# Other streamed weight blocks in a recurrent attention kernel, and six late weight loads on another queue

## The chip, the core and the metric

The kernel runs on one core of a Trainium2 chip. The metric is the time of the whole program on the device, in microseconds. The core has a matrix engine (TensorE, PE), a vector engine (VectorE, DVE), an engine for activations and copies (ScalarE, ACT), a general engine (GpSimd, POOL) and one that mainly issues transfers (SyncE, SP). Each engine works through its own queue in order; between engines, semaphores say when something is ready. Transfers from and to the device memory are started by SP or by GpSimd and carried by 16 DMA engines that all queues share.

## What is computed

Two attention blocks read the same input x of 2048 rows and 640 columns, and a gate mixes them. Block A is ordinary sliding-window attention. Block B is recurrent: it goes through the sequence in 64 segments of 32 rows, and each segment needs 8 rows of memory that the segment before it produced. Cut to what matters:

```python
mem = mem0                                  # 8 rows
for s in range(64):
    h = concatenate([mem, x[:, 32 * s:32 * s + 32]])        # 40 rows
    q, k, v = h @ Wq, h @ Wk, h @ Wv        # 640 -> 32 heads x 192, each
    p = softmax(mask(q @ k.T * 192 ** -0.5))
    o = (p @ v) @ Wo                        # 32 x 192 -> 640
    mem = o[:, :8]
    outs.append(o[:, 8:])
b = concatenate(outs)
out = g * A(x) + (1 - g) * b                # g = sigmoid(sum(x * gate_w))
```

The weights Wq, Wk, Wv and Wo are 640 x 6144 or 6144 x 640 in bfloat16, some 7.9 MB each. All four together do not fit in the core's on-chip memory, and every one of the 64 steps needs all of them.

## The kernel before

The program has three parts. First `branch_A` computes the sliding-window block, and while it does, some weights of block B are loaded. Then a tail part (`Tail`) computes q, k and v for 8 of each segment's rows ahead of time (the steps carry 32 rows, 8 of memory and 24 of the segment); the results are stored to a scratch tensor `xin` and read back step by step. Last, `branch_B` runs the 64 recurrent steps, and these take most of the time.

Weights are cut in blocks named (kind, g, m). The kind is q, k, v or o; g from 0 to 3 is a group of 8 heads; m counts the slices of the contraction: 5 for q, k and v (384 KB a block), 6 for o (320 KB a block). That makes 84 blocks. The table `STREAMED` (L1077) says for each kind and group which m are streamed: these 22 blocks are loaded anew in every step, into a ring of six buffers (`RING`, tile `b_w`). The other 62 are resident: loaded once and kept. Among the resident ones, in the order of a list, the first 24 are loaded during `branch_A`, the next 27 during the tail part, and the last 11 very late (`LAST`): five of them at the end of the tail part, and six, called `held`, in step 0 of `branch_B` by `load_slow` (L757). All eleven are of kind o. The first five of the six `held` blocks go into the tile `hold`, which the tail part used to stage its stores; the sixth goes into a tile of its own. A block of o with m % 3 = 1 lies in two pieces in memory and takes two DMAs (L545 and L546), any other takes one.

A step runs in an order written out by hand in `STEP` (L636): `k0` stands for the five chunks of k, group 0, one for each m; `tk0` turns the result by transposes; `s0` are the scores of the group, `p0` turns the probabilities, `pv0` multiplies them with v, `oa0` and `ob0` are the first three and last three chunks of the output projection, and `m` turns the new memory rows for the next step. A chunk (L794, L989) is four matmuls on one block, and a chunk on a streamed block has to wait for its landing. TensorE follows `STEP` word for word. SP issues the loads of the streamed blocks in the order in which their chunks stand in `STEP`. A load can go out only when its ring buffer is free, that is when the block six places earlier in that order has been used.

The other engines' orders come from a planner, `Sched` (L420). Each operation is given to it with an engine, an estimated duration and latency, and what it reads and writes; at each point the planner takes the ready operation with the longest chain of work behind it. `sc.op("SP", ...)` and `sc.op("POOL", ...)` thus set in which queue an instruction goes out; on SP the order is that of creation.

GpSimd issues small loads in each step: `b_xg` (rows of q and k from `xin`, one a group), `b_xv`, `b_hT` and `b_ga`; it issues the stores of the results; and it copies pieces of `b_xg` into the tiles `b_QT`, `b_K` and `b_Kz`, which the scores read (L831, L850, L852).

In step 0 `load_slow(g)` is called just before the chunks of `v` of group g are created, and loads those `held` blocks that belong to group g. So nothing is loaded at v0 and v1, two blocks at v2, and four at v3, all on SP's queue.

Of the kernel before, what the change touches and what calls it, by code (L numbers as in the profile page):

```python
# [416 lines left out]
D = 640  # L417
# [273 lines left out]
def branch_B(ctx, tc, xin, mem0, weights, ring, c, omg_sb, ga_dram, b_dram, outf, hold, held, rest):  # L691
    nc = tc.nc
# [14 lines left out]
    sc = Sched({"rest": len(held)} | {t: n for t, (n, _) in sb.items()} | {t: n for t, (n, _) in kept.items()} | ps)  # L707
# [47 lines left out]
    slow = {}  # L755

    def load_slow(g):  # L757
        for i, u in enumerate(held):
            if u[1] == g:
                b = slow[u] = sc.buf("rest")  # L760

                def f(i=i, u=u):
                    if i < HOLD:
                        weights.load_held(hold, i, u, nc.sync)
                    else:
                        weights.load_resident(rest, u, nc.sync)
                sc.op("SP", 0.753 * 2 * D, 3000, f, writes=[b])

    hts = {0: load_x(0)}
    tp, m0 = sc.buf("tr"), sc.buf("w")  # L770
# [2 lines left out]
    def f_m0():  # L773
        t = tile_of(tp, [P, KT, MEM], BF, "tp0")
        for kt in range(KT):
# [4 lines left out]
          writes=[hts[0][0]], after=[hts[0][1]])  # L780
    made, tails = {}, {}

    def chunk(kind, s, g):
        if s == 0 and kind == "v":
            load_slow(g)
        hT = hts[s][0]
        b = sc.buf("mm")
        wb = pieces(kind, g)

        def f(kt):  # L790
            t = tile_of(b, [P, 512], FP32, f"ps_{kind}")
            w = w_of(kind, g, kt, wb)
            for j in range(4):
                nc.tensor.matmul(t[32 * j:32 * j + 32, 0:384], lhsT=tile_of(hT)[:, kt, :], rhs=w[:, j * 384:(j + 1) * 384],  # L794
                                 start=(kt == 0), stop=(kt == KT - 1), tile_position=(0, 32 * j))
        for kt in range(KT):
            sc.op("PE", 160, 330, lambda kt=kt: f(kt), reads=[hT] + [wb[m] for m in wb if m == kt], writes=[b], name=(kind, s, g, kt), mode=32)
        tok = sc.buf("vtok" if kind == "v" else "tok")

        def ev():  # L800
            src, dst = b["tile"][:, 0:384], tile_of(tok)[:]
            if kind == "v":
                src = src.rearrange("p (a e b) -> p a b e", a=2, b=3)
                dst = dst.rearrange("p (a b e) -> p a b e", a=2, b=3)
            nc.scalar.copy(dst, src)  # L805
        sc.op("ACT", 480, 50, ev, reads=[b], writes=[tok])
        made[kind, s, g] = tok
# [248 lines left out]
    with tc.manual_schedule():  # L1056
        parts = []
        for n in names:
# [15 lines left out]
LAST = 11  # L1074
HOLD = 5
DENSE = 8
STREAMED = {"q": ((1,), (2,), (0,), (0,)),  # L1077
            "k": ((1,), (1,), (1,), (1,)),
            "v": ((3,), (0, 4), (1, 4), (0, 4)),
            "o": ((2, 3), (2,), (2, 3), (2, 5))}  # L1080


@with_exitstack
def kernel(
# [31 lines left out]
    allp = [(k, g, m) for k in KINDS for g in range(4) for m in range(6 if k == "o" else 5)]  # L1116
    streamed = [(k, g, m) for k, g, m in allp if m in STREAMED[k][g]]
    weights = Weights(tc, B_Wq, B_Wk, B_Wv, B_Wo, streamed)
# [131 lines left out]
```

## Time and profile before

| | |
|---|---|
| median of 14 runs | 2013.04 us (2008.72 to 2022.04) |
| the profiled execution | 2015.26 us, its span on the core 2013.6 us |
| TensorE busy | 1907.2 us, 95% of the span |
| VectorE, ScalarE, GpSimd busy | 1011.6, 949.3, 719.5 us |
| moved by DMA | 618.99 MB, 307 GB/s over the span |
| queue of SP (q1), its share of the 16 DMA engines' time | 565.28 MB, 78.1% |
| queue of GpSimd (q0) | 47.74 MB, 8.1% |
| streamed blocks: issue to landing, median | 5.2 us (v and o), 5.8 us (q and k) |
| granted TensorE clock | 0.998 |

The profile is of one execution. The span runs from the first instruction to the last; the run's own time has 1.7 us around it. In a row of matmuls the first number after the bar is the busy time and the second the mean time of one in ns; "idle before" is the engine's idle time ahead of the row's instructions, with what ended it. Matmuls overlap in TensorE's pipeline and their ends are modelled, so a short wait can vanish from the idle column; the distance between two start times cannot. "DMA share" is the mean busy share of the 16 DMA engines.

### The profile page before, as it was taken

The numbers are of one execution on the slowest core, as the hardware profiler recorded it, in microseconds if no ns is written. First come the engines' busy times: TensorE is split into PE (matmuls) and PEld (weight loads), VectorE is DVE, ScalarE is ACT, GpSimd is POOL, SyncE is SP. The second block draws the span as 40 slices with busy tenths as digits, with TensorE's granted clock in tenths as the row PEclk, the third lists the DMA queues.
The fourth block names the chain that finished last, engine by engine and source line by source line (L and its number), as shares of the span: only waits on it lengthen the run. The fifth ranks groups of instructions, "written<-read, shape, count | busy, mean of one in ns | idle before, by whom it ended". The sixth has DMA issues, their size and how long they took to land.

```text
span 2013.6 us, 92179 instructions
## 1 busy us (share of the span) xinstructions
PE 1907.2 (95%) x39590; PEld 1412.0 (70%) x39590; DVE 1011.6 (50%) x3338; ACT 949.3 (47%) x1951; POOL 719.5 (36%) x2006
## 2 busy tenths in 40 slices
PE   8999999989999999999999999999999999999998
PEld 6878878656677666666666677777666666666665
DVE  5777853334444444444444444444444444444444
ACT  4888832334444444444444444444444444444443
POOL 5111121233334333333434333433333333333432
PEclk9999999999999999999999999999999999999999
DMA  4222159789999999999999999999999999999997
GB/s 156 79 83 78 35 148 325 213 300 341 345 365 364 358 344 352 352 353 344 360 357 358 338 355 360 365 360 357 360 356 350 353 353 341 342 361 355 362 348 270
DMA packets 260401, 618.99 MB, mean 307 GB/s; under 512 B 40552, under 2 KB 60176, under 8 KB 259984
## 3 DMA queue, kind: packets, MB, share of 16 engines
q1 hardware_dynamic: 228560, 565.28, 78.1%
q0 software_dynamic: 31424, 47.74, 8.1%
q8 instruction: 312, 5.11, 1.0%
q14 instruction: 105, 0.86, 0.1%
HBM read 583.49 MB, written 29.37 MB: 304 GB/s over the span
## 4 chain that ended last, share of the span: by engine, by line
PE 72%; DMA 20%; DVE 3%; ACT 2%; issue 1%; SPq 0%; POOL 0%; ACTq 0%; POOLq 0%; DVEq 0%
PE ps_o L989 14%; PE ps_q L794 10%; PE ps_k L794 10%; PE ps_v L794 9%; DMA b_w<-in_B_Wo_dram 8%; DMA b_w<-in_B_Wk_dram 5%; PE t_psum L605 5%; DMA b_w<-in_B_Wv_dram 4%; PE S_ps L874 3%; PE t_psv L623 3%; PE tr_q L818 2%; PE qk_ps L155 2%; PE tr_k L818 2%; DMA b_w<-in_B_Wq_dram 2%; PE ps_pv L956 2%; PE s_ps L251 2%
## 5 line engine op out<-in xcount | busy, mean ns | idle before, releaser
L794 PEld LDWEIGHTS <-b_hT 128*32 128x32 bf16 x15360 | 369.0, 96 | 237.4 <-issue 39.8
L989 PEld LDWEIGHTS <-b_OT 128*64 128x64 bf16 x6144 | 379.3, 110 | 38.2 <-issue 25.0
L794 PE MATMUL ps_k<-w_k,b_hT 128*32 128x384 bf16 x4096 | 256.6, 327 | 4.4 <-issue 1.2
L794 PE MATMUL ps_q<-w_q,b_hT 128*32 128x384 bf16 x4096 | 235.4, 327 | 1.5 <-issue 1.4
L989 PE MATMUL ps_o<-hold,b_OT 128*64 128x320 bf16 x2560 | 224.9, 300 | 0.2 <-issue 0.2
L989 PE MATMUL ps_o<-b_w,b_OT 128*64 128x320 bf16 x1792 | 207.5, 300 | 16.0 <-DMA b_w<-in_B_Wo_dram 14.6
L845 DVE TENSOR_TENSOR b_Kz<-tr_k,marks 128x256 bf16<-128x256 bf16 x256 | 108.0, 422 | 222.9 <-PE tr_k L818 218.8
L940 DVE TENSOR_TENSOR b_PTm<-PT_ps,marks 128x320 bf16<-128x320 f32 x256 | 125.9, 492 | 178.7 <-PE PT_ps L928 178.7
L254 ACT ACTIVATE pt<-s_ps 128x1024 bf16<-128x1024 f32 x180 | 183.3, 1026 | 47.8 <-PE s_ps L251 46.2
L967 ACT CAST b_OT<-ps_pv 128x480 bf16<-128x480 f32 x256 | 143.1, 559 | 126.0 <-PE ps_pv L963 126.0
L805 ACT CAST b_tok<-ps_k 128x384 bf16<-128x384 f32 x256 | 122.6, 479 | 168.1 <-PE ps_k L794 159.7
L794 PE MATMUL ps_v<-w_v,b_hT 128*32 128x384 bf16 x3328 | 201.7, 327 | 0.0
L805 ACT CAST b_vtok<-ps_v 128x384 bf16<-128x384 f32 x256 | 122.7, 479 | 130.9 <-PE ps_v L794 129.2
L989 PE MATMUL ps_o<-w_o,b_OT 128*64 128x320 bf16 x1792 | 171.4, 300 | 0.6 <-issue 0.6
L739 POOL DMA_DIRECT2D b_xg<-xin x256 | 142.3, 556 | 83.1 <-POOL b_QT L831 54.6
L827 ACT COPY b_QT<-tr_q 128x384 bf16<-128x384 bf16 x256 | 123.4, 482 | 88.2 <-PE tr_q L818 86.4
L805 ACT CAST b_tok<-ps_q 128x384 bf16<-128x384 f32 x256 | 123.0, 481 | 87.6 <-PE ps_q L794 87.2
L794 PE MATMUL ps_v<-b_w,b_hT 128*32 128x384 bf16 x1792 | 152.5, 330 | 9.6 <-DMA b_w<-in_B_Wv_dram 8.9
L850 POOL COPY b_K<-b_xg 128x64 bf16<-128x64 bf16 x256 | 60.9, 238 | 279.5 <-PE S_ps L874 278.8
L1018 DVE CAST b_hT<-mem_ps 128x16 bf16<-128x16 f32 x126 | 22.5, 178 | 262.2 <-PE mem_ps L1012 258.9
L1035 POOL DMA_DIRECT2D out_dram<-b_ga x126 | 62.7, 498 | 244.5 <-DVE b_ga L1030 233.9
L818 PEld LDWEIGHTS <-b_tok 128*64 128x64 bf16 x3072 | 108.3, 110 | 43.6 <-issue 27.3
(150 smaller groups left out, 3696.7 us busy)
## 6 DMA issues: line engine op xcount, KB each, us to landing
b_w<-in_B_Wv_dram SPq DMA_DIRECT2D x448, 384.0 KB, 5.2
b_w<-in_B_Wo_dram SPq DMA_DIRECT2D x448, 320.0 KB, 5.2
b_w<-in_B_Wk_dram SPq DMA_DIRECT2D x256, 384.0 KB, 5.8
b_w<-in_B_Wq_dram SPq DMA_DIRECT2D x256, 384.0 KB, 5.8
xin<-hold POOLq DMA_DIRECT2D x8, 1536.0 KB, 12.3
b_xg<-xin POOLq DMA_DIRECT2D x256, 48.0 KB, 4.9
w_q<-in_B_Wq_dram SPq DMA_DIRECT2D x16, 384.0 KB, 3.6
w_k<-in_B_Wk_dram SPq DMA_DIRECT2D x16, 384.0 KB, 3.6
```

Of the source, the lines that this page charges most:

```text
L254: nc.scalar.activation(out=pt, in_=sp[:], func=ACT.Exp, scale=scale)
L605: self.nc.tensor.matmul(pt[:, bb, :], lhsT=w[kt][:, c:c + P], rhs=self.xTb[:, kt, t0:t0 + hs * MEM], start=(kt == 0), stop=(kt == KT - 1))
L739: sc.op("POOL", 540, 5000, lambda: nc.gpsimd.dma_start(tile_of(b)[:].rearrange("p i b t -> p (i b t)"), xin[s, :, c:c + 192]), writes=[b])
L794: nc.tensor.matmul(t[32 * j:32 * j + 32, 0:384], lhsT=tile_of(hT)[:, kt, :], rhs=w[:, j * 384:(j + 1) * 384], start=(kt == 0), stop=(kt == ...
L805: nc.scalar.copy(dst, src)
L818: nc.tensor.transpose(t[64 * a:64 * a + 64, k, :], tok["tile"][:, c:c + 64], ident[:], tile_position=(0, 64 * a))
L827: nc.scalar.copy(dst, tq["tile"][:].rearrange("p b (j t) -> p b j t", t=SEG))
L845: nc.vector.tensor_tensor(out=tile_of(Kz)[:, :, :, 0:SEG], in0=src, in1=mk_z.unsqueeze(1).unsqueeze(3).to_broadcast([P, 4, 2, SEG]), op=AL ...
L940: nc.vector.tensor_tensor(out=tile_of(PTm)[:], in0=src.to_broadcast([P, 2, 4, L]), in1=mk_m.unsqueeze(1).unsqueeze(3).to_broadcast([P, 2, ...
L967: sc.op("ACT", 560, 50, lambda: nc.scalar.copy(tile_of(OT)[:, 0:12 * L], o["tile"][:, 0:12 * L]), reads=[o], writes=[OT])
L989: nc.tensor.matmul(t[64 * h:64 * h + 64, 0:D // 2], lhsT=OT["tile"][:, c:c + 64], rhs=w, start=(g == 0 and m == 0 and n == 0), stop=(g == ...
L1035: sc.op(eng, 500, 3000, lambda h=h: queue.dma_start(half(outf, h), mine(tile_of(ga), h)), reads=[ga])
```

## The change

Two edits. The table of streamed blocks gets other entries. There are 22 a step before and after, of which q now has 6 (4 before), k 3 (4), v 6 (7) and o 7 (7). And `load_slow` puts the six held blocks on GpSimd's queue instead of SP's: three of them when v0 is created and three when v1 is, each after the last operation that was created before it; the estimates given to the planner change with it. As the table of o changes, the six held blocks are (o,2,3), (o,2,4), (o,3,0), (o,3,1), (o,3,3) and (o,3,4); before, they were (o,2,4), (o,2,5) and the same four of group 3.

```diff
     def load_slow(g):
-        for i, u in enumerate(held):
-            if u[1] == g:
-                b = slow[u] = sc.buf("rest")
-
-                def f(i=i, u=u):
-                    if i < HOLD:
-                        weights.load_held(hold, i, u, nc.sync)
-                    else:
-                        weights.load_resident(rest, u, nc.sync)
-                sc.op("SP", 0.753 * 2 * D, 3000, f, writes=[b])
+
+        half = -(-len(held) // 2)
+        last = sc.ops[-1]
+        for i, u in list(enumerate(held))[g * half:(g + 1) * half]:
+            b = slow[u] = sc.buf("rest")
+
+            def f(i=i, u=u):
+                if i < HOLD:
+                    weights.load_held(hold, i, u, nc.gpsimd)
+                else:
+                    weights.load_resident(rest, u, nc.gpsimd)
+            sc.op("POOL", 560, 6000, f, writes=[b], after=[last])
...
-STREAMED = {"q": ((1,), (2,), (0,), (0,)),
-            "k": ((1,), (1,), (1,), (1,)),
-            "v": ((3,), (0, 4), (1, 4), (0, 4)),
-            "o": ((2, 3), (2,), (2, 3), (2, 5))}
+STREAMED = {"q": ((4,), (3,), (1, 4), (0, 3)),
+            "k": ((1,), (4,), (), (4,)),
+            "v": ((2,), (4,), (1, 4), (0, 4)),
+            "o": ((0, 3), (2,), (2, 5), (2, 5))}
```

## The prediction

> **What bounds the kernel now.** I read the page's slices first, then the chain of waits, then the windows of single steps, then TensorE's order of time inside a step.
>
> ```profile
> DMA  4222159789999999999999999999999999999997
> GB/s 156 79 83 78 35 148 325 213 300 341 345 365 364 358 344 352 352 353 344 360 357 358 338 355 360 365 360 357 360 356 350 353 353 341 342 361 355 362 348 270
> ...
> PE 72%; DMA 20%; DVE 3%; ACT 2%; issue 1%; SPq 0%; POOL 0%; ACTq 0%; POOLq 0%; DVEq 0%
> ...
> L989 PE MATMUL ps_o<-b_w,b_OT 128*64 128x320 bf16 x1792 | 207.5, 300 | 16.0 <-DMA b_w<-in_B_Wo_dram 14.6
> ```
>
> From slice 9 on, the 64 recurrent steps run: TensorE and the DMA engines are both full, and the chain goes over PE with 20% on the landings of b_w, the streamed weight blocks. Four windows give step 0, steps 1 and 2, and a step in the middle:
>
> ```profile
> core 0: us, PE busy (x) PEld busy (x) DVE busy (x) ACT busy (x) POOL busy (x), PEclk, DMA share, GB/s
> 420.00:450.60 30.60, 24.72 (x521) 17.51 (x521) 11.19 (x41) 11.53 (x26) 8.57 (x28) 0.94 1.00 363
> 450.60:475.90 25.30, 23.51 (x526) 16.92 (x526) 11.83 (x43) 11.01 (x25) 9.65 (x28) 1.00 0.98 347
> ...
> 1018.60:1043.00 24.40, 23.61 (x526) 16.49 (x526) 11.82 (x43) 10.59 (x24) 9.66 (x28) 1.00 0.99 352
> ```
>
> The idle column understates the waits, because matmul ends are modelled. The start times show them:
>
> ```profile
> 1020.38 0.66 PE L794 MATMUL ps_q<-w_q,b_hT 128*32 128x384 bf16 x12
> 1020.87 0.34 PE L794 MATMUL ps_k<-w_k,b_hT 128*32 128x384 bf16 x4
> 1021.32 0.35 PE L794 MATMUL ps_k<-b_w,b_hT 128*32 128x384 bf16 x4
> 1021.48 0.67 PE L794 MATMUL ps_k<-w_k,b_hT 128*32 128x384 bf16 x12
> ```
>
> A chunk of four matmuls follows the one before it after 0.16 us; the chunk on b_w, k(1,1), came after 0.45: 0.29 us of waiting with no idle time in the row. I measured every chunk so, start to start, over steps 2 to 63, against its own 5th percentile. A step has a mean of 24.68 us: a floor of **23.43** (all 5th percentiles), **0.89** lost ahead of the 22 streamed chunks, 0.36 elsewhere. The fastest five steps took 23.7. So 0.89 x 63 = 56 us is all that block placement could ever give.
>
> **Part 1: the streamed blocks at other places.** Bytes first: both tables stream 15 blocks of 384 KB and 7 of 320 KB a step, and none of the o blocks streamed in either has m % 3 = 1, so one DMA each. SP issues the same 22 DMAs, in the order of use. What changes is the spacing. Block i can be issued only when block i-6 has been used, so its time is the PE time between these two uses, its **window**. From the issue (about 0.25 us after the use ends) to the landing takes 5.2 to 5.8 us by the median, 3.7 at least: a window under about 6 has little to spare. I laid both tables on the floor's times (a chunk 0.163, of o 0.272 us). Per place: window before > after, and the block's measured slack (landing to use, median) with the mean wait before:
>
> - o(2,3) > o(2,5): 5.18 > 5.72; slack 0.04, wait 0.247
> - k(1,1) > k(1,4): 5.92 > 6.40; 0.06, 0.150
> - v(3,4) stays: 5.57 > 6.12; 0.28, 0.079
> - v(2,4) stays: 5.53 > 6.02; 0.47, 0.067
> - o(1,2) stays: 5.38 > 6.24; 0.52, 0.029
> - q(0,1) > q(0,4): 6.09 > 6.57; 0.61, 0.037
> - q(1,2) > q(1,3): 6.82 > 6.44; 0.63, 0.045
> - k(2,1) > q(2,4): 7.24 > 6.51; 1.18, 0.010
> - k(3,1) > q(3,3): 7.17 > 6.20; 1.29, 0.014
> - v(1,0) > k(3,4): 6.97 > 5.95; 1.53, 0.005
> - o(2,2), o(3,5), o(3,2), k(0,1) keep 5.83, 5.56, 6.04, 5.93; waits 0.059, 0.067, 0.001, 0.025
>
> The rest keeps a slack near 1. I add the change of window to the slack and read the new wait off the same list (slack 0.5 to 0.6 went with about 0.03, 0.3 with about 0.07). Gains: o(2,5) 0.22, k(1,4) 0.12, v(3,4) 0.07, v(2,4) 0.06, o(1,2) and q(0,4) 0.03 each: 0.53. Losses: q(1,3) at slack 0.25 0.035, q(2,4) at 0.45 0.04, q(3,3) at 0.32 0.055, k(3,4) at 0.51 0.035: 0.165. Net **-0.37 us a step if the windows were independent**.
>
> They aren't: a wait that goes also shortens the windows that held it. 0.37 us less per step is 0.37 x 6/22 = 0.10 us less in each window. Nine places then stand under 0.6 of slack; near there the list loses about 0.25 us of wait per us of slack: 9 x 0.10 x 0.25 = +0.22. What is left is **-0.15 us a step, x 63 = -9 us**. Ends: no feedback, -23; all given back because the transfers are the bound, 0. I take -9.
>
> A rule speaks against any gain. The Trainium skill, page "DMA: Bandwidth & Descriptors", section "Bandwidth" (Where 436 GB/s comes from), says that loads from HBM are held by a limit of about 358 GB/s per core. Slices 10 to 38 average 354 GB/s, which over 24.68 us is 8.74 MB a step; at 358 the step could not go below 24.4, a gain of at most 0.27 us a step, 17 in all. The trace goes past it: slices reach 365, and a 384 KB block that had a backlog ahead of it landed 0.97 us after its predecessor by the median, 405 GB/s. By the row the floor stays PE's 23.43. My -9 fits under both; the far end is -17 by the rule and -23 by the row. The row decides, but I let the rule pull the low end in a little.
>
> **Part 2: the late loads.** Six late o blocks (1.97 MB, nine DMAs, as three have m % 3 = 1) went out on SP ahead of the ring loads of v2 and v3 in step 0:
>
> ```profile
> 436.97 0.35 PE L794 MATMUL ps_v<-b_w,b_hT 128*32 128x384 bf16 x4 [1.20 <-DMA b_w<-in_B_Wv_dram]
> 438.07 0.35 PE L794 MATMUL ps_v<-b_w,b_hT 128*32 128x384 bf16 x4 [0.43 <-DMA b_w<-in_B_Wv_dram]
> 443.43 0.35 PE L794 MATMUL ps_v<-b_w,b_hT 128*32 128x384 bf16 x4 [2.58 <-DMA b_w<-in_B_Wv_dram]
> 444.71 0.51 PE L794 MATMUL ps_v<-b_w,b_hT 128*32 128x384 bf16 x4 [0.28 <-DMA b_w<-in_B_Wv_dram]
> ```
>
> That is 4.49 us of waiting, of the 5.35 by which step 0 (30.03) exceeds the mean. On GpSimd's queue they no longer stand ahead of ring loads in one queue, and are issued some 2 us earlier, at v0 and v1. But six blocks of 320 KB take 6 x 0.83 = 5.0 us of the DMA engines (0.83 is the landing distance of such blocks), and the window of step 0 above shows a DMA share of 1.00: there is no hole to put them in. The two queues' packets will mix, ring loads run slower while both are full, and the waits spread over o(0,3), v(2,4), o(1,2) and v3 with the same sum. So **0**, between -4.5 (all hidden) and +5 (late and doubled).
>
> SP is rid of nine issues of 0.33 to 1.2 us. GpSimd takes them on, four behind the evacuation of k2 and five behind the copies of tk2, each near this row:
>
> ```profile
> L739 POOL DMA_DIRECT2D b_xg<-xin x256: 537/556/581, 304.7 to 1988.3; - x128
> ```
>
> 9 x 0.556 = 5.0 us of GpSimd, once. Behind them stand its copies of xg into K02, Kz and QT, which S of the next group reads; GpSimd waited 1.5 to 3.9 us for S_ps before each group of copies in step 0, so four or five issues (2.2 or 2.8 us) are mostly covered. Without that cover: +2 us. The skill's page "SBUF — State Buffer", section "SBUF: two separate sides", warns of exactly this move: descriptors of a GpSimd DMA wait for VectorE's two-port instructions, 620 ns becoming 3100. By it the nine would take 28 us and starve the scores of step 0, about +15. The row says no: 256 issues beside a VectorE busy 47% of a step took 581 ns at most. I take the row. The destination (hold) was last read by stores issued at 421.8 at the latest, which land some 4.3 us later, before 428, so that wait costs nothing.
>
> What lies ahead of step 0 moves one q and one v block between ring and resident loads with equal bytes: 0, +/-1.
>
> **Sum**, against the profiled execution (span 2013.6, 2015.26 with what lies around it): -9 + 0 + about 1 for GpSimd = -8. The median of 14 runs, 2013.04, is 2.2 below that execution; taken off the median: **2005**.
>
> **Rivals.**
> - *A, the transfers are the bound* (share 0.98 to 0.99 in each step): bytes equal, so every wait removed returns elsewhere. For it: the share. Against it: steps of 23.7 us happen. Time: 2013, +/-4.
> - *B, no feedback*: -0.37 x 63 = -23, cut to -19 by the bandwidth: 1994. Against it: landings have a backlog in most cases, so slack is shared.
> - *C, slower: the new crowd in q2 to k3.* q(2,1), q(2,4), v(0,2), q(3,0), q(3,3), k(3,4) pull six blocks into 4.9 us of PE time where five stood, and two pairs are 0.5 us apart while a block takes 0.97. xg, out and ga transfers of GpSimd pass in the same stretch. If q(2,4), q(3,3) and k(3,4) each wait as k(1,1) did (0.15) and feedback takes half of the gain, the step is 3 x 0.15 + 0.035 - 0.53/2 = +0.22 worse before its own feedback, some +0.1 after: 2019. It decides from a mean wait of about 0.12 at each of the three.
> - That the step table does nothing is excluded: SP and PE read it directly.
>
> **Chances.** The likeliest case 0.50, A 0.25, B 0.08, C 0.17. Its own range is 1998 to 2011. For 8 in 10 I go from 1995 (most of B) to 2016 (A, the edge of C). A measurement here tells 0.2%, 4 us, from nothing. Faster: 0.45 of the likeliest, B, and a little of A: 0.57; same 0.26; slower 0.17.
>
> **What would show it.** Right: mean step near 24.5, waits ahead of o(2,5) and k(1,4) under 0.06, total ahead of streamed chunks near 0.74, step 0 again near 30 but with its waits smaller and more of them; nine GpSimd issues near 0.55 us. Wrong: waits over 0.12 at q(2,4), q(3,3), k(3,4) (C); a mean step at 24.7 with waits moved to o(2,2) and o(3,5) (A); GpSimd issues over 1 us or S_ps waiting for GpSimd in step 0; step 0 under 28 or over 33 us.

## The result, and the profile after

The changed kernel takes 1997.66 us (median of 10 runs, 1989.93 to 2002.47); the kernel before, run beside it, 2012.87. The ratio is **0.9921**, 95% interval 0.9904 to 0.9938: 15 us, 0.8% faster. The forecast was 2005, 8 us faster.

The page of the changed kernel (lines after L757 have moved by two: L794 is L796 now, L989 is L991). First the chain of waits by engine, then two groups of matmuls on streamed blocks:

```profile
PE 77%; DMA 14%; DVE 3%; ACT 2%; issue 2%; SPq 0%; POOL 0%; ACTq 0%; POOLq 0%; DVEq 0%
...
L991 PE MATMUL ps_o<-b_w,b_OT 128*64 128x320 bf16 x1792 | 205.9, 300 | 0.9 <-DMA b_w<-in_B_Wo_dram 0.7
...
L796 PE MATMUL ps_q<-b_w,b_hT 128*32 128x384 bf16 x1536 | 130.9, 329 | 9.8 <-DMA b_w<-in_B_Wq_dram 8.3
```

The row of the q chunks before:

```profile
L794 PE MATMUL ps_q<-b_w,b_hT 128*32 128x384 bf16 x1024 | 87.5, 332 | 3.1 <-DMA b_w<-in_B_Wq_dram 2.9
```

Landings fell from 20% of the chain to 14%. The o chunks on streamed blocks waited 16.0 us in the row of before and 0.9 now; the q chunks, of which half as many again are streamed, waited 3.1 and now 9.8. The list of waits has a second place where the same loss stands, and it is easily misread: weight loads (PEld) that waited for "issue", that is for nothing the profile names. Before (who waited for what: us in total, times, longest):

```profile
PEld L794 <- issue: 39.8, 84, 1.7
...
PEld L989 <- issue: 25.0, 51, 1.7
```

After:

```profile
PEld L796 <- issue: 44.1, 83, 2.0
...
PEld L991 <- issue: 4.3, 11, 0.8
```

I looked up which matmul follows each of these waits from step 1 on: of 64.8 us on both lines before, 53.8 stand directly ahead of a chunk on b_w; of 48.4 after, some 34. I take these for late landings too, seen at the weight load instead of the matmul; with half the bytes (below) they are gone. For o they have nearly gone (25.0 to 4.3), for q, k and v they have not.

Start to start, which counts both kinds, as in the prediction (steps 2 to 63, each chunk against its own 5th percentile, us a step):

| | mean step | floor | ahead of streamed chunks | elsewhere | step 0 |
|---|---|---|---|---|---|
| before | 24.68 | 23.43 | 0.89 | 0.36 | 30.03 |
| after | 24.43 | 23.41 | 0.55 | 0.47 | 31.64 |

62 steps x 0.25 = 15.7 us less; step 0 is 1.6 longer, step 1 1.2 shorter, and the part ahead of step 0 0.8 shorter: together 16.1 of the 16.3 by which the profiled span shrank (2013.6 to 1997.3). So in these two executions the whole gain lies in the steady steps.

Step 0 is another picture. The windows of steps 0 and 1 of the changed kernel, with the columns of the prediction's:

```profile
420.30:452.00 31.70, 25.52 (x530) 17.80 (x531) 11.39 (x42) 11.09 (x25) 12.88 (x34) 0.95 0.97 354
452.00:476.10 24.10, 23.17 (x529) 16.77 (x530) 11.81 (x44) 11.00 (x25) 9.61 (x29) 1.00 0.98 345
```

GpSimd is busy for 12.88 us in step 0 (8.57 before), and the DMA share has fallen from 1.00 to 0.97. TensorE's order of time says why; these two starts follow waits that the kernel before did not have:

```profile
433.56 0.21 PE L876 MATMUL S_ps<-b_K,b_QT 128*64 128x40 bf16 x2 [0.82 <-POOL b_QT L833]
...
439.78 0.21 PE L876 MATMUL S_ps<-b_K,b_QT 128*64 128x40 bf16 x2 [2.33 <-POOL b_QT L833]
```

And GpSimd's order of time, where the bracket is its idle time:

```profile
430.93 0.55 POOL L542 DMA_DIRECT2D hold<-in_B_Wo_dram  x1 [4.02 <-issue]
...
435.34 0.54 POOL L542 DMA_DIRECT2D hold<-in_B_Wo_dram  x1
435.86 0.54 POOL L545 DMA_DIRECT2D w_o<-in_B_Wo_dram  x1
437.17 0.54 POOL L546 DMA_DIRECT2D w_o<-in_B_Wo_dram  x1 [0.77 <-DMA hold<-in_B_Wo_dram]
438.22 0.54 POOL L739 DMA_DIRECT2D b_xg<-xin  x1 [0.52 <-DVE b_PTm L942]
438.75 0.25 POOL L852 COPY b_K<-b_xg 128x64 bf16<-128x64 bf16 x1
438.92 0.48 POOL L854 COPY b_Kz<-b_xg 64x32 bf16<-64x32 bf16 x2
439.46 0.26 POOL L833 COPY b_QT<-b_xg 128x96 bf16<-128x96 bf16 x1
```

The scores of group 3 needed the copies at 437.4; they stood behind six issues, the last of the first half and the five of the second, and behind a load of xg; TensorE waited until 439.78. In the kernel before, the late loads went out on SP from here on:

```profile
429.16 0.33 SPq L545 DMA_DIRECT2D hold<-in_B_Wo_dram  x1
```

### The profile page after: what moved, and what is told of

Same layout as the page of the kernel before. It is cut to its first block, busy times and chain, and to the rows that moved or that the text cites. A ratio compares the mean times of both kernels' runs of the same rounds, so it can differ in the third digit from the quotient of the medians.

```text
span 1997.3 us, 92168 instructions
## 1 busy us (share of the span) xinstructions
PE 1899.5 (95%) x39590; PEld 1398.9 (70%) x39590; DVE 1011.6 (51%) x3338; ACT 949.0 (48%) x1951; POOL 721.9 (36%) x2015
## 4 chain that ended last, share of the span: by engine, by line
PE 77%; DMA 14%; DVE 3%; ACT 2%; issue 2%; SPq 0%; POOL 0%; ACTq 0%; POOLq 0%; DVEq 0%
PE ps_o L991 19%; PE ps_v L796 10%; PE ps_q L796 9%; PE ps_k L796 9%; DMA b_w<-in_B_Wq_dram 6%; PE t_psum L605 4%; DMA b_w<-in_B_Wv_dram 4%; PE S_ps L876 3%; PE ps_pv L958 3%; PE t_psv L623 3%; PE qk_ps L155 3%; PE tr_q L820 2%; DMA b_w<-in_B_Wk_dram 2%; PE tr_k L820 2%; PE s_ps L251 2%
## 5 line engine op out<-in xcount | busy, mean ns | idle before, releaser
L796 PEld LDWEIGHTS <-b_hT 128*32 128x32 bf16 x15360 | 372.6, 96 | 242.6 <-issue 44.1
L991 PEld LDWEIGHTS <-b_OT 128*64 128x64 bf16 x6144 | 363.0, 111 | 30.9 <-ACT b_OT L969 9.6
L796 PE MATMUL ps_k<-w_k,b_hT 128*32 128x384 bf16 x4352 | 235.3, 328 | 3.6 <-issue 0.4
L991 PE MATMUL ps_o<-hold,b_OT 128*64 128x320 bf16 x2560 | 236.1, 301 | 0.5 <-issue 0.5
L796 PE MATMUL ps_q<-w_q,b_hT 128*32 128x384 bf16 x3584 | 224.5, 328 | 0.5 <-issue 0.5
L796 PE MATMUL ps_v<-w_v,b_hT 128*32 128x384 bf16 x3584 | 213.7, 328 | 4.3 <-issue 2.1
L991 PE MATMUL ps_o<-b_w,b_OT 128*64 128x320 bf16 x1792 | 205.9, 300 | 0.9 <-DMA b_w<-in_B_Wo_dram 0.7
L739 POOL DMA_DIRECT2D b_xg<-xin x256 | 141.8, 554 | 89.1 <-POOL b_QT L833 53.8
L991 PE MATMUL ps_o<-w_o,b_OT 128*64 128x320 bf16 x1792 | 169.4, 299 | 0.4 <-issue 0.4
L893 ACT ACTIVATE S_ps<-S_ps 128x160 f32<-128x160 f32 x256 | 75.1, 294 | 137.6 <-DVE S_ps L890 136.6
L796 PE MATMUL ps_q<-b_w,b_hT 128*32 128x384 bf16 x1536 | 130.9, 329 | 9.8 <-DMA b_w<-in_B_Wq_dram 8.3
```

The costliest lines, as they stand in the source:

```text
L739: sc.op("POOL", 540, 5000, lambda: nc.gpsimd.dma_start(tile_of(b)[:].rearrange("p i b t -> p (i b t)"), xin[s, :, c:c + 192]), writes=[b])
L893: nc.scalar.activation(out=view(), in_=view(), func=ACT.Exp, scale=scale)
L991: nc.tensor.matmul(t[64 * h:64 * h + 64, 0:D // 2], lhsT=OT["tile"][:, c:c + 64], rhs=w, start=(g == 0 and m == 0 and n == 0), stop=(g == ...
```

## The experiments

The theory: the gain comes from the table alone, by the windows; the moved loads bring nothing. The rivals: the loads carry part of it; the transfers are the bound and placement only moves the waits. All ratios are to the kernel before on the same chip, with their 95% intervals. In a profile of one execution the mean step varies by some 0.1 us, so medians decide, and the places only show where. How far one profile carries can be seen where two kernels have the same table (us a step, as in the table above; e8 is the changed kernel with another queue for the late loads):

| | table | mean step | floor | ahead of streamed chunks | elsewhere |
|---|---|---|---|---|---|
| before | old | 24.68 | 23.43 | 0.89 | 0.36 |
| e2 | old | 24.72 | 23.44 | 0.99 | 0.29 |
| changed | new | 24.43 | 23.41 | 0.55 | 0.47 |
| e1 | new | 24.59 | 23.37 | 0.82 | 0.40 |
| e8 | new | 24.44 | 23.33 | 0.55 | 0.56 |

The direction is the same in all: the mean of the three minus the mean of the two is -0.22 us a step, of which -0.30 ahead of streamed chunks, +0.15 elsewhere and -0.07 in the floor. The size of a single term is not: e1's execution took 8 us more than its median. Its row of the o chunks has 5.3 us of waiting where the changed kernel has 0.9, a third of the 16.0 before:

```profile
L989 PE MATMUL ps_o<-b_w,b_OT 128*64 128x320 bf16 x1792 | 205.8, 300 | 5.3 <-DMA b_w<-in_B_Wo_dram 4.4
```

The part ahead of step 0 varies too, without any difference in the program: it took 420.4 us in e7 and 426.1 in the same kernel again.

**The table alone**, and **the loads alone**. The change is taken apart at its seam; in e1 `load_slow` is as before, in e2 the table is:

```diff
 e1:  "o": ((2, 3), ...) -> ((0, 3), (2,), (2, 5), (2, 5)), q, k, v likewise
 e2:  nc.sync -> nc.gpsimd in load_slow, as in the change
```

> The new table of streamed blocks alone, the late loads on SP's queue as before. Windows theory (the waits are set by the spacing of the uses, and all of the gain comes from the table): mean step near 24.43 us as after, streamed waits near 0.55 a step, step 0 back near 30.0 instead of 31.6, with no wait of the scores for GpSimd's copies; about 1996 us, ratio 0.9915 to the kernel before. Rival (the moved loads carried part of the gain): slower than the changed kernel, over 2000 us.

> The late loads on GpSimd's queue alone, the old table. Windows theory: step 0 near 31.6 us with the scores of groups 2 and 3 waiting for GpSimd's copies, all later steps as before (24.7), so 1 to 2 us slower than before, near 2014.5. Rival (the moved loads carried part of the gain): faster than before by 3 us or more.

The table alone: 1999.61 us, ratio 0.9925 (0.9900 to 0.9949), the same as the whole change. The loads alone: 2013.53, ratio 0.9993 (0.9978 to 1.0008), no difference that can be told. Step 0 was 30.53 and 30.83 us. In e2 the scores waited again for GpSimd, 1.05 and 1.37 us:

```profile
435.00 0.21 PE L876 MATMUL S_ps<-b_K,b_QT 128*64 128x40 bf16 x2 [1.05 <-POOL b_QT L833]
...
440.27 0.21 PE L876 MATMUL S_ps<-b_K,b_QT 128*64 128x40 bf16 x2 [1.37 <-POOL b_QT L833]
```

The rival that the loads carry part of the gain falls. The 1 to 2 us of loss that e2 was to show are below what these intervals resolve.

**Only the o row**, and **only the q, k and v rows** of the new table, loads on SP:

```diff
 e3:  q, k, v as before; "o": ((0, 3), (2,), (2, 5), (2, 5))
 e4:  q, k, v as after;  "o": ((2, 3), (2,), (2, 3), (2, 5))
```

> Only the o row of the new table; loads on SP. Windows theory: o(2,3)'s wait of 0.25 us goes (o(2,5) below 0.05), v(3,4) falls from 0.08 to 0.02, but q(1,2) loses 0.54 us of window (6.82 to 6.28) and waits about 0.15; net -0.15 to -0.2 us a step before other places take some back, so -6 to -10 us. Rival A (the transfers are the bound): the step stays at 24.7, the waits appear elsewhere, 0 +/- 3 us.

> Only the q, k and v rows of the new table; loads on SP. Windows theory: k(1,4) waits 0.03 to 0.05 instead of 0.15, v(2,4) and o(1,2) little, q(2,4) about 0.17 as after, o(2,3) still about 0.25, net -0.1 us a step, -4 to -7 us; with e3 it adds up to the -15 us of the whole table. Rival A: 0 +/- 3 us. If the places share one pool of slack, e3 and e4 each give clearly more, or less, than their part of the sum.

The o row alone: 2002.68 us, ratio 0.9934 (0.9912 to 0.9956). The other three rows: 2014.43, ratio 0.9994 (0.9976 to 1.0013). Eight of the ten moved blocks bring nothing together that can be told (5 us less to 3 us more); the two o blocks bring nearly everything. The profile of e4 shows the balance that the theory expected, at smaller sizes: k(1,4) waits 0.06 (k(1,1) had 0.15), q(2,4) 0.10 (k(2,1) had 0.01), and o(2,3) still 0.16. Its -4 to -7 us were too much. That the new o blocks merely load faster than those that they replace can be excluded: in the changed kernel, o blocks with a backlog ahead of them landed 0.90, 0.86, 0.82 and 0.82 us after their predecessor for m = 0, 2, 3 and 5 (medians).

**One o block at a time**:

```diff
 e10: "o": ((2, 3), (2,), (2, 5), (2, 5))      # o(2,3) to o(2,5)
 e11: "o": ((0, 3), (2,), (2, 3), (2, 5))      # o(0,2) to o(0,0)
```

> One block alone is moved: o(2,3) to o(2,5), everything else as before. Windows theory with little feedback (a wait that goes stays gone): the 0.2 to 0.25 us ahead of o(2,3) vanish, q(1,2) loses 0.54 us of window and keeps some slack, so the step gets 0.15 to 0.2 us shorter, -9 to -13 us, nearly all that the whole table brought. With the feedback of the prediction (0.6 of each gain given back elsewhere): -4 to -6 us. Rival (several places share the gain, v(3,4) by the release of o(0,0) among them): under half of the -12.6 us of the whole o row.

> One block alone is moved: o(0,2) to o(0,0), everything else as before. It releases its ring buffer 0.55 us earlier for v(3,4), whose window grows from 5.57 to 6.12; its own window falls from 6.25 to 5.71. The whole o row gave -12.6 us and o(2,5) alone -4.2. Windows theory: v(3,4) stops waiting (0.08 to 0.02) and lands earlier, so o(2,2) and o(2,3) behind it in the DMA queue land earlier too; -0.1 us a step, -4 to -8 us, and the two edits add up. Rival (they do not add up; o(0,0) alone does nothing): 0 +/- 3 us.

Both ratios are 0.9979 (0.9964 to 0.9995, and to 0.9993): 4 us each, 1 to 7. So by the medians o(2,3), with a wait of 0.25 us a step (16 us in all) the worst place of the kernel before, yielded about a quarter of that when it was moved alone. The profile of e10 does not bear out so much feedback: its waits did go to the last o places (o(2,5) 0.055, o(3,2) 0.052, o(3,5) 0.054), but its mean step is 24.50, 0.18 less than before, which is 11 us over 62 steps; its part ahead of step 0 took 426.5 us, 5.3 more than before. How much one place gives back when it is moved alone is therefore not settled. The sum of the two, 0.42%, with 0.15% of uncertainty on each, lies just below the interval of e3 (0.44 to 0.88%); whether the two help each other beyond their sum is not settled.

e11 missed in a way that teaches more than its time. Moving o(0,2) to o(0,0) let v(3,4) be issued 0.56 us earlier (6.04 us ahead of its use by the median, 5.48 before), and I expected its wait to go. But its time from issue to landing rose by the same amount, 5.23 to 5.80 us, its slack stayed (0.28 to 0.31), and the mean wait ahead of it was 0.13 us (0.08 before). Here the earlier issue only meant a longer wait in a queue that still had blocks ahead.

**Half the bytes.** The kernel before, where each streamed block is loaded by half and its chunk reads that half twice; half of the streamed weights is left out of the computation.

```diff
-                sc.op("SP", ..., lambda b=b, u=u: weights.load(u, tile_of(b)[:, 0:weights.width(u[0])], nc.sync), writes=[b])
+                sc.op("SP", ..., lambda b=b, u=u: weights.load_half(u, tile_of(b), nc.sync), writes=[b])
...
+                i = j % 2 if kt in wb else j      # q, k, v: which quarter is read
```

> The kernel before, but each streamed block is loaded by half only and its chunk reads this half twice; so half of the streamed weights is left out, while SP's issues, TensorE's instructions and the ring are the same. Windows theory: landings come 2 to 3 us after the issue, all waits ahead of streamed chunks vanish, the mean step is the floor and the 0.36 to 0.47 us of other waits, 23.8 to 23.9: about 1958 us. That would be the most that any placement can give. Rival (the steps are held by something else than landings, say PE's issue or the copies of other engines): over 24.3 us a step, over 1985.

1944.59 us, ratio 0.9677 (0.9643 to 0.9711): 68 us less, more than expected. The waits ahead of streamed chunks are 0.01 us a step, as the theory has it. What I had not expected: the waits elsewhere fell too, from 0.36 to 0.11 us, and the mean step is 23.63, close to the floor. Landings come 2.8 us after the issue by the median (5.4 before), and no wait for "issue" is left on the lines of the weight chunks; what TensorE's weight loads keep of it stands mainly in three rows, on lines that read no streamed block:

```profile
PEld L936 <- issue: 20.6, 65, 0.3
...
PEld L877 <- issue: 20.4, 64, 0.3
...
PEld L828 <- issue: 20.4, 64, 0.3
```

So about 1.05 us of each step of the kernel before hangs on the streamed bytes, not 0.89.

**Five ring buffers**, with the new table, loads on SP:

```diff
-RING = 6
+RING = 5
```

> The new table with five ring buffers, loads on SP. The bytes are the same; each window loses about 1.07 us (a fifth of a step's spacing). Windows theory: the median slack of 0.4 to 1.2 us is gone at nearly all places, waits of 0.3 us and more at half of them, the step grows by 1 to 2 us: 2065 to 2125. Rival A (the transfers are the bound at 24.4 us a step, and placement only decides where one waits): under +15 us, below 2015.

2108.47 us, ratio 1.0462 (1.0430 to 1.0494): 94 us slower with the same bytes, within what the windows foretold; against e1, from which only the ring differs, it is 5.4% by the two ratios. The mean step is 26.08, of which 2.42 us are ahead of streamed chunks. Here is the same stretch of the run with five buffers, and of that with half the bytes (columns as before: PE, PEld, DVE, ACT, POOL busy, clock, DMA share, GB/s). Five buffers:

```profile
1000.00:1050.00 50.00, 45.86 (x1022) 32.38 (x1020) 23.08 (x84) 21.19 (x48) 18.51 (x55) 1.00 0.96 335
```

Half the bytes:

```profile
1000.00:1050.00 50.00, 48.76 (x1129) 35.40 (x1127) 25.99 (x96) 23.47 (x53) 20.77 (x61) 1.00 0.69 197
```

Rival A read the share of 0.98 as a transfer system at its end. With five buffers the share is still 0.96 while only 335 GB/s are moved and TensorE waits for a tenth of the step. In steady steps this share cannot tell a full queue from a starved kernel. So what rival A rested on does not hold it up. It falls by e1: the same bytes, and 15.6 us less. The ring of five adds that shorter windows alone, at equal bytes, cost time. A ring of seven was not tried.

**Another queue for the late loads**: the changed kernel with ScalarE's queue in place of GpSimd's.

```diff
-                    weights.load_held(hold, i, u, nc.gpsimd)
+                    weights.load_held(hold, i, u, nc.scalar)
...
-            sc.op("POOL", 560, 6000, f, writes=[b], after=[last])
+            sc.op("ACT", 60, 6000, f, writes=[b], after=[last])
```

> The changed kernel, with the six late loads on ScalarE's queue instead of GpSimd's. If step 0 is held by the bytes (a DMA share near 1), it stays at 30 to 31 us: the waits of the scores for GpSimd's copies (0.8 and 2.3 us in the changed kernel) vanish, and waits for landings take their place; total within 2 us of the changed kernel and of e1. If it is held by the order within a queue, step 0 falls to 27 to 28 us and the total by 3 to 4.

2002.16 us, ratio 0.9947 (0.9929 to 0.9965), against 0.9921 for the changed kernel. Neither case came: step 0 is 33.28 us. The scores no longer wait for GpSimd, but ScalarE's queue stood while its loads waited to go out, and its evacuations behind them with it. ScalarE, then TensorE:

```profile
432.11 0.33 ACTq L545 DMA_DIRECT2D hold<-in_B_Wo_dram  x1
433.27 0.34 ACTq L546 DMA_DIRECT2D hold<-in_B_Wo_dram  x1
434.80 0.33 ACTq L542 DMA_DIRECT2D hold<-in_B_Wo_dram  x1
435.90 0.33 ACTq L545 DMA_DIRECT2D w_o<-in_B_Wo_dram  x1
436.27 0.46 ACTq L546 DMA_DIRECT2D w_o<-in_B_Wo_dram  x1
436.77 0.48 ACT L807 CAST b_tok<-ps_q 128x384 bf16<-128x384 f32 x1 [6.64 <-DMA hold<-in_B_Wo_dram]
...
437.30 1.47 PE L796 MATMUL ps_v<-w_v,b_hT 128*32 128x384 bf16 x16 [6.84 <-ACT b_tok L807]
```

TensorE waited 6.84 us for that cast. What the loads waited for can be read off the trace: each of the four from 432.11 to 435.90 went out 0.02 to 0.16 us after the landing of an earlier load that had used the same semaphore (431.95, 433.20, 434.72, 435.88). In this program the loads of SP and ScalarE draw on the same set of semaphores, so another queue did not let more of them be under way. SP, where nothing but loads stands, was the best of the three: step 0 took 29.8 to 30.5 us in all variants with the loads on SP and six whole blocks in the ring, 30.8 and 31.6 in the two with GpSimd's queue.

**Two other tables.** e7 takes the worst place of the changed kernel away, the pair q(2,1), q(2,4); e13 makes the windows as even as I could. Loads on SP in both.

```diff
 e7:  q2 (1, 4) -> (0,), k2 () -> (1,), else the new table
 e13: "q": ((2,), (3,), (0,), (1,)), "k": ((0,), (4,), (1, 3), (4,)),
      "v": ((4,), (0,), (0, 4), (0, 4)), "o": ((0, 2), (2,), (2,), (0, 3, 5))
```

> The new table with q2 = (0,) and k2 = (1,) in place of q2 = (1, 4) and k2 = (), loads on SP. Windows theory: the pair q(2,1), q(2,4), only 0.49 us apart, is gone and with it the 0.12 to 0.17 us ahead of q(2,4); o(0,0) keeps a window of 5.71 and may wait up to 0.07; the step gets 0.05 to 0.1 us shorter than with the new table, -3 to -6 us against it, near 1995. Rival (a shared pool of slack): 1999.6 as e1.

> The kernel of e7 once more, beside e13. Windows theory: again near 0.9913 of the kernel before, 2 to 8 us below the new table's 0.9921 and 0.9925. Rival (the first time was chance): 0.9925 or more.

> A table made for even windows: at least 5.56 us, and 6.1 or more over the whole last third of the step, q ((2,), (3,), (0,), (1,)), k ((0,), (4,), (1, 3), (4,)), v ((4,), (0,), (0, 4), (0, 4)), o ((0, 2), (2,), (2,), (0, 3, 5)); loads on SP. Windows theory: the waits in v3 and o, the largest in the kernel before, are as small as with the new table or smaller, waits spread over v0, q3, v1 (windows 5.8 to 5.9): near 1993, within 5 us of e7. Rival (the pair k(2,1), k(2,3), 0.33 us apart, waits as q(2,4) did): 1998 to 2004.

e7: 1992.17 us, ratio 0.9913 (0.9885 to 0.9941), and again 1995.57, ratio 0.9906 (0.9885 to 0.9928). Its profiles have 0.41 and 0.45 us ahead of streamed chunks (0.55, 0.82 and 0.55 in the three with the new table), and steps of 24.27 and 24.33. It is faster than the kernel before both times, and both times a little below the changed kernel, but their intervals overlap and they were not run side by side; that it beats the changed kernel is likely, not shown. e13: 1999.2, ratio 0.9931 (0.9909 to 0.9954). The last third of its step waits almost nowhere (o(3,0) and o(3,3) 0.001), but its own tight pair, k(2,1) and k(2,3), 0.33 us apart, waits 0.12 at k(2,3), as q(2,4) had done: the rival of its expectation, in place and in time.

## Why the prediction was right, and where its sizes were off

- **Direction and place: right.** Bytes equal, gain in the steady steps, by the waits ahead of streamed chunks; e1 and e2 show it came from the table alone. The forecast had 8 us less, the medians show 15: 1997.66 lies just below the likeliest case's own range (1998 to 2011) and nearer to rival B, no feedback, at 1994.
- **The size, -9 us by the table: too small; measured about -16 (e1, by the medians), -15.7 in the steady steps of the profile.** The term that does not fit is the feedback, +0.22 us a step. It was to grow at nine places under 0.6 of slack, among them those that kept their windows, o(2,2), o(3,2) and o(3,5), which were to wait more. They waited less: 0.02, 0.07 and 0.09 us together in the three profiles with the new table, 0.13 and 0.14 in the two with the old. Their blocks also landed sooner after the issue (5.59 to 5.38, 5.60 to 5.28 and 5.32 to 4.81 us by the median, with much the same in e1 and e8). A likely reason, argued and not tested alone, is that neighbours share one queue of landings: with several blocks spread at once the next ones land earlier as well. What was given back came elsewhere, where the sum had nothing: ahead of o(1,0) 0.05 to 0.07 us (0.02 before) and ahead of o(2,3), which is no longer streamed, 0.06. In the one pair of profiles 0.11 came back of 0.34, over all five 0.15 of 0.30; so where the feedback falls was wrong in the sum, and how large it is the profiles do not settle.
- **"I add the change of window to the slack": wrong as a step.** v(2,4) was issued 0.49 us earlier and gained 0.11 of slack, o(1,2) 0.87 and 0.26, v(3,4) 0.44 and 0.33; in e11 v(3,4) gained nothing for 0.56. The window sets when a block may go out, the queue ahead of it when it lands.
- **The places.** Foretold wait and measured one: o(2,5) 0.03, 0.00; v(3,4) 0.01, 0.02; o(1,2) 0, 0.01; k(1,4) 0.03, 0.05; v(2,4) 0.01, 0.08 (no gain); q(1,3) 0.08, 0.04; q(2,4) 0.05, 0.17 (0.12 and 0.09 in e1 and e8); q(3,3) 0.07, 0.02; k(3,4) 0.04, 0.02. Rival C had the right place once of three times: q(2,4), the one that stands 0.49 us behind its neighbour with the smallest slack.
- **The rule on 358 GB/s.** The measurement sides with the row, as taken: e7's mean step was 24.27 us, a little below the 24.4 that the rule gave, single steps of it took 23.56 with the same bytes, and slices of the changed kernel reach 369 GB/s.
- **Part 2, the late loads: the sum was near, its working was not.** Foretold 0 for the bytes and about +1 for GpSimd; step 0 became 1.6 us longer, of which the table alone (e1) had 0.5. That the sum came near was luck. The loads were to be issued some 2 us earlier: the first went out at 430.93, 4.02 us after GpSimd's last work and later than the 429.16 on SP. The 2.2 and 2.8 us of issues were to be "mostly covered"; the copies behind them made the scores wait 0.82 and 2.33 us. The price of an issue was right (0.54 to 0.55 us, none near 3.1), so the rule on descriptors and VectorE does not show here. The last store that reads `hold` took 6.0 us to land in the kernel before (421.76 to 427.75), not 4.3, which is still before 428. The statement that would prove the part wrong, the scores waiting for GpSimd, came true.
- **The sum of part 1's ceiling.** 56 us were said to be all that placement could give; with half the bytes 68 us went, since waits elsewhere hang on the same load and step 0 shrinks too.

## What to carry to other kernels

Where a ring of buffers feeds an engine that consumes at a fixed pace, look at the distance between consecutive uses as well as at the distance over the whole ring. The worst places behind the change were second blocks of close pairs: q(2,4), 0.49 us behind its neighbour, and in e13 k(2,3), 0.33 behind, while blocks with a backlog land some 0.97 us apart. Closeness alone does not decide: q(3,3), 0.50 us behind q(3,0), waited only 0.02, for q(3,0) had 1.1 us of slack, and q(2,1), ahead of q(2,4), 0.8. So add the pair's distance to the slack of its first block and take off the 0.97 us between landings: that gives 0.3 for q(2,4), 0.6 for q(3,3) and 0.2 for k(2,3) in e13, where 0.15, 0.58 and 0.09 of slack were measured. Judge a table of places as a whole: in this kernel one block moved alone gave 4 us by the medians where its own wait was worth 16, two gave 13, and eight others together nothing that could be told. And put loads on a queue where nothing urgent stands behind them: GpSimd and ScalarE each held up work that TensorE needed, for 3 and 7 us, though for GpSimd the loss in the whole time is below what the medians resolve (e2).

## What was not expected of the hardware

The DMA share stayed at 0.96 with five buffers at 335 GB/s, against 0.98 to 0.99 with six at 350, so a share near 1 is no proof of a bound. Time from issue to landing fell from 5.4 to 2.8 us by the median when the blocks were halved, much more than the 0.5 us that half of a block's own 0.97 us accounts for. So most of it was time behind other transfers, and GpSimd's loads bear this out: those of xg, on another queue and of the same size in both kernels, landed 2.1 us sooner. Before, then with half the bytes (KB each, median us to landing):

```profile
b_xg<-xin POOLq DMA_DIRECT2D x256, 48.0 KB, 4.9
...
b_xg<-xin POOLq DMA_DIRECT2D x256, 48.0 KB, 2.8
```

And GpSimd idled 4.02 us ahead of the first late load in the changed kernel, 3.83 in e2, for nothing that the profile names. It was not the last store that reads `hold`, which had landed at 427.19 in the changed kernel; what held it is open.
